# Fused attention and two gated layers on one core: three pairs' first products with v in full fp32, the first pair loaded in one transfer per part, and a new order for attention

## The chip, the cores and the metric

The kernel runs on one core of a Trainium2 chip. The metric is the device time of one execution in microseconds (us), lower is better. It is taken as the median of several runs. The engines are named as in the profile: PE is TensorE (matmuls), PEld its weight loads, DVE is VectorE, ACT is ScalarE, POOL is GpSimd, and SP is SyncE, which here issues nearly all DMA transfers.

## The reference

Attention with a threshold, then a gated layer, then a layer with a cosine:

```
# q, k, v: (batch 4, heads 8, sequence 576, head width 64), fp32
scores = q @ k.T / 8
scores = where(scores >= rowmax(scores) - tau, scores, -1e9)
attn   = exp(scores - rowmax(scores)); attn /= rowsum(attn) + 1e-9
x      = attn @ v                          # laid out as 2304 tokens x 512
x      = (sigmoid(x @ w_gate) * (x @ w_val)) @ w_out      # width 1536
h      = x @ w_in                                          # width 2048
out    = (h * cos(h)) @ w_out2
```

The layers' weights arrive as float64, and the kernel turns their words into fp32 itself.

## The kernel before, in words

Almost every product is made from operands that are split in two: a high part that is rounded to the matmul's own fp32r form, and a low part, which is what the rounding left. High by high, high by low and low by high are then summed in PSUM, so that the result is close to full fp32 without a full fp32 matmul.

**Attention** goes over 16 pairs of heads. For each pair there are nine blocks of 128 query rows, written `Queries` in the code: four blocks of 128 rows for each of the two heads, and one block that joins the last 64 rows of both heads. A block goes through these tasks, each with a letter in the order strings:

- S: PE makes the scores of 128 rows by 576 keys (two or three matmuls for each half of 288 columns).
- M, E, Y, K: DVE takes the row maximum, ACT the exponential, some engine adds the threshold (`YS` says which), DVE masks and sums.
- T and t: PE transposes the result in pieces of 128 by 128, since the product with v wants the keys on the partitions.
- H and h: ACT copies the transposed piece out of PSUM as the high part. H is 512 wide, h is 128 or less.
- the low part, in one of three ways, which `LOWS` and `LOWS_L` choose for each piece. "V": DVE subtracts the high part from PSUM (L, l). "G": ACT copies the piece once more (C), and POOL subtracts (G). "T": PE subtracts the high part inside PSUM by a matmul with minus the identity (N, n), and ACT copies what is left (O, o).

A pair's products with v (`Values`, letter V) come in two blocks of queries (blk 0 with 256 columns, blk 1 with 320) for each of the two heads. Each sums over five slots of 128 keys. Two forms exist, and `SHARED` chooses. In the plain one the high and low columns of v stand side by side in the array, which takes 9 matmuls and leaves two halves that ACT folds (F) and DVE adds (A). In the shared one ("S") they are added in PSUM in 14 matmuls, and one ACT copy (a) takes the result. The fifth slot needs the rest keys' high and low parts stacked on the partitions: four DMA transfers from SP (s) do that. v itself is loaded by SP (2) and split into high and low by Z and z.

When a pair's products are done, x is divided by the row sums (U), stored, and split (X, x). As soon as two pairs of one batch are through, the first layer's products for that batch can begin (letter P, 144 tasks): they are what PE does between the blocks of later pairs.

**The order** of all these tasks on each engine is written out by hand in `ORDER`, one string for each engine. The first pair is loaded by a way of its own (`begin`): q in three parts and k in two, each part by two transfers that put the same rows into the lower and the upper 64 partitions. Before the first scores PE transposes the identity 36 times (`warm`), and four-transpose fillers (letter D, `FILL`) follow a few of the first blocks.

**The layers** follow from about 386 us on; their order is not touched by the change.

## Time and profile before

| | |
|---|---|
| runs | 1092.18, 1090.88 and 1091.71 us: median 1091.71 |
| profiled execution | 1094.26 us, of which the span from first to last instruction is 1092.5 |
| granted TensorE clock | 1.000 over the span |
| PE busy | 1071.8 us, 98% |
| DVE busy | 909.9 us, 83% |
| ACT busy | 764.4 us, 70% |
| POOL busy | 543.7 us, 50% |

The span is about 1.8 us shorter than the profiled execution's own time: that is what lies before the first and after the last instruction. The profiled execution is 2.55 us above the median of the runs. The busy time of PE is modelled from the starts of matmuls that overlap, so a stretch in which PE is 98% busy can still hold small gaps. Attention takes the first 386 us or so, and the two layers the other 706 us.

### The profile page before, as it was taken

The numbers are of one execution on the slowest core, as the hardware profiler recorded it, in microseconds if no ns is written. First come the engines' busy times: TensorE is split into PE (matmuls) and PEld (weight loads), VectorE is DVE, ScalarE is ACT, GpSimd is POOL, SyncE is SP. The second block draws the span as 40 slices with busy tenths as digits, with TensorE's granted clock in tenths as the row PEclk, the third lists the DMA queues.
The fourth block names the chain that finished last, engine by engine and source line by source line (L and its number), as shares of the span: only waits on it lengthen the run. The fifth ranks groups of instructions, "written<-read, shape, count | busy, mean of one in ns | idle before, by whom it ended". The sixth has DMA issues, their size and how long they took to land.

```text
span 1092.5 us, 17726 instructions
## 1 busy us (share of the span) xinstructions
PE 1071.8 (98%) x5784; PEld 912.5 (84%) x5784; DVE 909.9 (83%) x1647; ACT 764.4 (70%) x1488; POOL 543.7 (50%) x521
## 2 busy tenths in 40 slices
PE   8899999999999999999999999999999999999998
PEld 7788898888888888988888888888888888888886
DVE  7999898999888747877787657788779899889998
ACT  6999788887888744656554334367876777788774
POOL 6867877746675525232335252242244535445563
PEclk9999999999999999999999999999999999999999
DMA  7888788787777278998877554866444444557752
GB/s 194 235 225 250 213 225 225 205 232 216 198 207 203 90 231 280 329 331 315 299 228 244 163 191 138 291 203 210 173 154 154 157 175 169 193 193 262 277 203 87
DMA packets 94494, 234.06 MB, mean 214 GB/s; under 512 B 13258, under 2 KB 21570, under 8 KB 84674
## 3 DMA queue, kind: packets, MB, share of 16 engines
q1 hardware_dynamic: 94242, 232.60, 66.7%
q8 instruction: 46, 0.75, 0.3%
q10 hardware_dynamic: 160, 0.33, 0.1%
q14 instruction: 46, 0.38, 0.1%
HBM read 141.33 MB, written 59.84 MB: 184 GB/s over the span
## 4 chain that ended last, share of the span: by engine, by line
PE 51%; DVE 2%; DMA 1%; ACT 1%; issue 0%; ACTq 0%
PE h L1441 5%; PE h L1442 5%; PE h L1443 5%; PE h L1630 4%; PE h L1631 4%; PE h L1632 4%; PE o L1750 4%; PE o L1751 4%; PE o L1752 4%; PE o L565 3%; PE o L566 3%; PE o L564 3%; DMA early<-gd 1%; PE o L1840 1%; PE o L1842 1%; PE o L1841 1%
## 5 line engine op out<-in xcount | busy, mean ns | idle before, releaser
L1676 POOL TENSOR_TENSOR g<-raws,g 128x512 fp32r<-128x512 f32 x68 | 94.7, 1402 | 139.7 <-ACT g L1675 117.6
L965 DVE TENSOR_REDUCE sm<-s 128x1 f32<-128x576 f32 x144 | 106.5, 751 | 8.9 <-PE s L959 7.2
L973 DVE SCALAR_TENSOR_TENSOR p<-s,sm,p 128x576 f32<-128x576 f32 x128 | 102.7, 812 | 9.3 <-ACT p L970 3.9
L1441 PE MATMUL h<-x,w 128*128 128x256 f32 (+1 forms) x304 | 101.4, 333 | 0.4 <-DVE raws L1718 0.4
L1442 PE MATMUL h<-x,w 128*128 128x256 f32 (+1 forms) x304 | 101.3, 333 | 0.0
L1443 PE MATMUL h<-x,w 128*128 128x256 f32 (+1 forms) x304 | 101.3, 333 | 0.0
L970 ACT ACTIVATE p<-s,sm 128x576 f32<-128x576 f32 x128 | 93.8, 742 | 9.8 <-DVE sm L965 9.0
L899 ACT ACTIVATE PT<-t 128x512 fp32r<-128x512 f32 (+1 forms) x160 | 86.1, 557 | 15.1 <-PE t L989 10.3
L959 PE MATMUL s<-kk,qh 128*128 128x288 f32 x320 | 92.4, 320 | 2.9 <-DVE p L973 2.5
L1056 PE MATMUL v<-PT,vn 128*128 128x256 f32 (+3 forms) x532 | 84.7, 302 | 0.2 <-ACT st L1214 0.2
L919 POOL TENSOR_TENSOR PT<-praw,PT 128x512 fp32r<-128x512 f32 x51 | 66.7, 1307 | 35.4 <-ACT praw L914 16.9
L1760 DVE TENSOR_TENSOR y<-o,y 128x512 f32<-128x512 f32 x120 | 78.6, 681 | 6.1 <-PE o L1752 5.9
L959 PE MATMUL s<-khi,ql 128*128 128x288 f32 x288 | 81.0, 295 | 0.6 <-DVE ql L670 0.6
L989 PE MATMUL t<-ident,p 128*128 128x128 f32 x512 | 77.0, 276 | 3.2 <-DVE PT L910 1.7
L1750 PE MATMUL o<-g,w 128*128 128x512 f32 x196 | 76.8, 392 | 0.5 <-ACT o L1766 0.5
L1751 PE MATMUL o<-g,w 128*128 128x512 f32 x196 | 76.4, 390 | 0.0
L1752 PE MATMUL o<-g,w 128*128 128x512 f32 x196 | 76.3, 389 | 0.0
L1630 PE MATMUL h<-form,w 128*128 128x512 f32 x192 | 75.0, 390 | 0.5 <-ACT side L1599 0.5
L1056 PEld LDWEIGHTS v<-PT,vn 128*128 128x128 f32 (+1 forms) x532 | 73.3, 186 | 2.2 <-DVE x L1031 0.5
L1631 PE MATMUL h<-form,w 128*128 128x512 f32 x192 | 74.7, 389 | 0.0
L1632 PE MATMUL h<-form,w 128*128 128x512 f32 x192 | 74.7, 389 | 0.0
L1675 ACT ACTIVATE g<-raws 128x512 fp32r<-128x512 f32 x106 | 64.3, 624 | 13.1 <-DVE raws L1718 8.3
(212 smaller groups left out, 3386.1 us busy)
## 6 DMA issues: line engine op xcount, KB each, us to landing
w<-wd SPq DMA_DIRECT2D x62, 1024.0 KB
wd<-stage SPq DMA_DIRECT2D x64, 512.0 KB
gd<-st SPq DMA_DIRECT2D x64, 256.0 KB
wraw<-in_moe_w_out_dram SPq DMA_DIRECT2D x28, 512.0 KB
qh<-qsplit SPq DMA_DIRECT2D x60, 144.0 KB
wraw<-in_moe_w_in_dram SPq DMA_DIRECT2D x16, 512.0 KB
spare<-gd SPq DMA_DIRECT2D x7, 1024.0 KB
early<-gd SPq DMA_DIRECT2D x7, 1024.0 KB
```

What stands on the lines that cost most here:

```text
L959: nc.tensor.matmul(s[:, half, 0:HALF], qq, keys[:, half * HALF:half * HALF + HALF], start=(i == 0), stop=(i == len(mms) - 1),)
L965: nc.vector.tensor_reduce(self.sm()[:, 0:1], self.s()[:, :, 0:HALF], axis=AX.XY, op=ALU.min)
L1056: nc.tensor.matmul(o, w, x, start=z == 0, stop=z == len(steps) - 1)
L1441: nc.tensor.matmul(o, w_hi, x(0, c), start=begin, stop=False, **late)
L1442: nc.tensor.matmul(o, w_hi, x(1, c), start=False, stop=False, **late)
L1443: nc.tensor.matmul(o, w_lo, x(0, c), start=False, stop=c == KC - 1, **late)
L1630: nc.tensor.matmul(ps(), of(0, c), hi, start=fresh and c == 0, stop=False, skip_group_check=True)
L1631: nc.tensor.matmul(ps(), of(0, c), lo, start=False, stop=False, skip_group_check=True)
L1632: nc.tensor.matmul(ps(), of(1, c), hi, start=False, stop=c == 1, skip_group_check=True)
L1750: nc.tensor.matmul(ps(), of(0, c), hi, start=begin, stop=False, skip_group_check=True)
L1751: nc.tensor.matmul(ps(), of(0, c), lo, start=False, stop=False, skip_group_check=True)
L1752: nc.tensor.matmul(ps(), of(1, c), hi, start=False, stop=True, skip_group_check=True)
```

## The change

- `SHARED` gets a third value, "F". The first two products of the first three pairs (blk 0, both heads) carry it. For them the transposed pieces are copied out of PSUM once, as plain fp32, and no low part is made. The product takes v as it was loaded, unsplit, and is made of five plain fp32 matmuls of 256 columns. It doesn't need the four stacking transfers, and its result is taken by one ACT copy, as in the shared form.
- The tile that v is loaded into gets a second buffer.
- Each part of the first pair's q and k is loaded by one transfer of 128 partitions, from a copy in DRAM that holds the rows twice.
- 26 identity transposes instead of 36 stand before the first scores. Half of the zero fills at the start go to DVE. The second copy of the first pair's keys on POOL waits for the first part of q's low half as well.
- `ORDER`, `LOWS`, `LOWS_L`, `SHARED`, `WHERE`, `YS` and `FILL` are new for all of attention. `WHERE` says for each pair which engine scales, splits and divides.

The count of tasks that change, before and after: PE N 18 to 4, n 3 to 2; ACT O 18 to 4, o 3 to 2, F 59 to 56, a 5 to 8, Y 29 to 36, X 4 to 7; DVE L 91 to 93, l 93 to 88, A 59 to 56, Y 53 to 60, U 2 to 6, q 4 to 6, z 1 to 2; POOL Y 62 to 48, U 15 to 11, X 12 to 9, q 14 to 12; SP s 124 to 112.

```diff
 LOWS = (
-    "TTGTTVTTG VTGVVTVVT GVTTVTGVT VGVVVVGGV GVVVGVTGV VVVGGVGVG GVVGVVGVG GVGVVVVGV "
...
+    "FFFFVTGVG FFFFGVVGT FFFFTVVGV VGVVVVGVV GGVVGVVGV VGVGGVGVG GVGVGVGVV GGVGVVGVV "
...
 LOWS_L = (
-    "TVVV VVTV VVVV VVVV VVVV VVVV VVVV VVVV VVTV VVVV VVVV VVVV VVVV VVVV VVVV VVVV "
+    "VVVT VVVV VVVV VVVV VVVV VVVV VVVV VVVV VVTV VVVV VVVV VVVV VVVV VVVV VVVV VVVV "
 SHARED = (
-    "SSS. .S.S .... .... .... .... .... .... .... .... .... .... .... .... .... .... "
+    "FF.. FF.S FF.. ...S .... .... .... .... .... .... .... .... .... .... .... .... "
 WHERE = dict(
-    Q="APPPPPPPPPAAAPPP", q="DPPPPPPPPPPPPDPP", J="APPPPPPPPAPPPPPP", j="DPPPPPPPPPPDPPPP",
-    Z="PPAPPPPPPPPPPAAP", z="PPPPPPPPPPPPPDPP", s="AAPPPPPPPAPAAPPP", X="PPPPPPPPPPPAAAPA", x="DDPPPPPPPPPPDDDD", U="PPPPPPPPPPPPPPPP",
+    Q="APPAPPPPPPPAPPPP", q="DPPPPDPPPPPDPDPP", J="APPPPPPAPPPPAPPA", j="DPPPDPPPPPPPPPPP",
+    Z="APPPAPPPPPPPPPPA", z="PPPPPDDPPPPPPPPP", s="AAAAPPPPPPPPPPAA", X="PAAPPPPPPAAPAAPA", x="PPPPPPPDDPPPDDDD", U="PDPPPPPPPPPDPDDP",
 YS = (
-    "APPPPDDDD DPPPPPPAA ADPAPADPA DPPDPPPPA PPPDPAPPA DDPDPADPP PPPDPDPDD ADPAAPDPD "
+    "DPPDPDDDA PPPPDDPPD PAPAAPPPP DDAADDDAP ADDPPADPD ADAPPDPDD PDDDDADAD AADAADAAP "
...
-            nc.gpsimd.memset(f32(t), 0.0)
+            (nc.vector if i else nc.gpsimd).memset(f32(t), 0.0)
...
-    for _ in range(36):
+    for _ in range(26):
         nc.tensor.transpose(warm[:, 0:P], ident, ident)
...
+        def exact(self, blk):
+            return SHARED[4 * self.p + 2 * blk] == "F"
...
         def load(self, nm, part=None, queue=nc.sync):
...
-                self.raw[nm] = at.tile([P, src.shape[1]], F32, tag=f"raw_{nm}", name=f"raw_{nm}")
+                self.raw[nm] = at.tile([P, src.shape[1]], F32, tag=f"raw_{nm}", name=f"raw_{nm}", bufs=2 if nm == "v" else 1)
                 queue.dma_start(self.raw[nm], src)
                 return
-            src = self.src[nm][NP].rearrange("(d a) n -> d (a n)", a=2)
-            for i in range(2):
-                queue.dma_start(self.first_raw(nm, part)[64 * i:64 * i + 64], src[:, part])
+            width = src.shape[1]
+            half = part.start // width
+            queue.dma_start(self.first_raw(nm, part), self.src[nm][NP + half][:, part.start - half * width:part.stop - half * width])
...
                 if nm == "k":
                     half["K", i] = task("POOL", pool1(S) + (0.24 if not i else 0.0), "J", lambda r=r: self.first_keys(r), last,
-                                        uses=[*raw, self.khi])
+                                        i and half["q", 0], uses=[*raw, self.khi])
...
             if blk not in pair.LT:
+                kind = F32 if pair.exact(blk) else F32R
...
                 last = task("ACT", act(size) + (0.13 if size < P else 0), high_, high, turn, uses=[bank, to])
-                if by == "G":
+                if pair.exact(blk):
+                    pass
+                elif by == "G":
...
-            self.LZ = pair.LT[blk] if self.close else pair.LZ[blk]
-            lasts = pair.last[blk] if self.close else pair.stacked[blk]
+            self.LZ = pair.LT[blk] if self.close or self.exact else pair.LZ[blk]
+            lasts = pair.last[blk] if self.close or self.exact else pair.stacked[blk]
...
+            if self.exact:
+                raw, steps = self.pair.raw["v"], [(4 * h + c, everything, PT[:, 0, c, 0:n]) for c in range(4)]
+                steps.append((8 + h, one_head, self.LZ()[one_head, 0, 0:n]))
+                for z, (slot, rows, x) in enumerate(steps):
+                    nc.tensor.matmul(o, raw[rows, D * slot - 64 * h:D * slot + D], x, start=z == 0, stop=z == len(steps) - 1)
+                return
```

## Rows read from the trace of the kernel before

**Rows 1.** The page: busy time of the engines, and the granted clock in 40 slices.

```profile
PE 1071.8 (98%) x5784; PEld 912.5 (84%) x5784; DVE 909.9 (83%) x1647; ACT 764.4 (70%) x1488; POOL 543.7 (50%) x521
...
PEclk9999999999999999999999999999999999999999
```

**Rows 2.** Busy us (and count) of PE, PEld, DVE, ACT, POOL by stretch.

```profile
8.00:73.70 65.70, 57.40 (x390) 48.77 (x389) 61.91 (x135) 58.95 (x129) 48.85 (x56) 1.00 0.83 223
73.70:386.00 312.30, 307.85 (x1994) 268.36 (x1993) 278.03 (x645) 263.67 (x574) 202.82 (x236) 1.00 0.73 205
...
386.00:1092.50 706.50, 699.90 (x3369) 588.75 (x3367) 567.97 (x864) 438.28 (x781) 286.35 (x212) 1.00 0.63 218
```

**Rows 3.** Timeline of the start: start, us, engine, instruction.

```profile
0.73 1.19 ACTq L640 DMA_DIRECT2D x<-in_k_dram  x2
...
1.18 1.19 SPq L640 DMA_DIRECT2D x<-in_q_dram  x2
...
1.36 5.51 PE L599 MATMUL warm<-ident 128*128 128x128 f32 x25 [1.36 <-POOL halfpi L477]
...
5.18 0.74 ACT L657 ACTIVATE kk<-x 128x640 fp32r<-128x640 f32 x1 [1.74 <-DMA x<-in_k_dram]
...
5.95 0.82 DVE L674 TENSOR_TENSOR kk<-x,kk 64x640 fp32r<-64x640 f32 x1 [2.33 <-ACT kk L657]
...
6.71 1.36 PE L599 MATMUL warm<-ident 128*128 128x128 f32 x11
...
6.80 0.73 DVE L670 SCALAR_TENSOR_TENSOR ql<-x,taus,qh 64x128 fp32r<-64x128 f32 x1
...
6.87 0.44 SPq L636 DMA_DIRECT2D raw_k<-in_k_dram  x1
...
7.83 0.38 PE L959 MATMUL s<-kk,qh 128*128 128x288 f32 x1
```

**Rows 4.** DVE's groups by form, 0 to 386 us: busy us, mean ns.

```profile
L910 DVE TENSOR_TENSOR PT<-t,PT 128x512 fp32r<-128x512 f32 x65 | 44.5, 685 | 5.8 <-ACT PT L899 5.0
L910 DVE TENSOR_TENSOR LT<-t,LT 128x128 fp32r<-128x128 f32 x61 | 17.2, 281 | 2.7 <-ACT LT L899 2.3
...
L1031 DVE TENSOR_TENSOR x<-v,half 64x256 f32<-64x256 f32 x29 | 12.1, 418 | 0.8 <-ACT half L1026 0.2
L817 DVE TENSOR_SCALAR sm<-sm,taus 128x1 f32<-128x1 f32 x53 | 10.6, 205 | 0.4
...
L910 DVE TENSOR_TENSOR PT<-t,PT 128x256 fp32r<-128x256 f32 x26 | 10.1, 419 | 3.1 <-ACT PT L899 2.8
...
L1169 DVE TENSOR_TENSOR xs_a<-x,xs_a 128x512 fp32r<-128x512 f32 x4 | 2.7, 681 | 0.0
...
L710 DVE TENSOR_TENSOR ql<-raw_q,qsplit 128x576 fp32r<-128x576 f32 x1 | 0.7, 748 | 0.0
```

**Rows 5.** ACT's copy of a T-form low part, 0 to 386 us.

```profile
L906 ACT ACTIVATE PT<-t 128x512 fp32r<-128x512 f32 x12 | 7.2, 599 | 0.1
```

**Rows 6.** Timeline of PE: fillers, one shared product, the first layer product.

```profile
8.44 1.91 PE L825 MATMUL warm<-ident 128*128 128x128 f32 x16
...
30.12 1.61 PE L1056 MATMUL v<-PT,vn 128*64 128x256 f32 x12
31.57 0.39 PE L1056 MATMUL v<-LZ,vn 128*64 128x256 f32 x2
31.80 0.39 PE L903 MATMUL t<-PT,minus_r 128*128 128x512 f32 x1
...
70.84 0.40 PE L564 MATMUL m<-xs_a,w 128*128 128x512 f32 x1
```

**Rows 7.** PEld's groups by form, 0 to 386 us: weight loads.

```profile
L989 PEld LDWEIGHTS t<-ident,p 128*128 128x128 f32 x512 | 59.0, 140 | 16.9 <-DVE PT L910 3.2 <-DVE LT L910 3.0 <-ACT PT L906 0.9
...
L1056 PEld LDWEIGHTS v<-PT,vn 128*64 128x64 f32 x24 | 3.0, 134 | 0.1
```

**Rows 8.** The chain of waits between 375 and 505 us, longest piece.

```profile
487.60 12.15 DMA early<-gd
```

More of the change, by code (lines that the diff above doesn't have):

```diff
@@ L126 @@
 FILL = (
-    "421001001 000000000 000000000 000000000 000000000 000000000 000000000 000000000 "
+    "421100010 000000000 000000000 000000000 000000000 000000000 000000000 000000000 "
     "000000000 000000000 000000000 000000000 000000000 000000000 000000000 000000000 "
@@ L724, in values @@
             p = self.p
-            raw = buf("raw_v")
+            raw = self.raw_v = buf("raw_v", size=2)
             eh, el = either("Z", p), either("z", p)
-            last = task("SP", 0.47, "2", lambda: self.load("v"), uses=[raw], moved=VW)
+            last = self.v_raw = task("SP", 0.47, "2", lambda: self.load("v"), uses=[raw], moved=VW)
             last = task(eh, act(VW, True) if eh == "ACT" else pool1(VW), "Z", lambda: self.hi("v", eh), last, uses=[raw, self.vb])
@@ L751, in begin @@
                 if (nm, i) not in (("q", 0), ("k", 0)):
-                    last = task("SP", 0.94, load, lambda nm=nm, r=r: self.load(nm, r), uses=raw, moved=n)
+                    last = task("SP", 0.57, load, lambda nm=nm, r=r: self.load(nm, r), uses=raw, moved=n)
                 if nm == "k":
                     half["K", i] = task("POOL", pool1(S) + (0.24 if not i else 0.0), "J", lambda r=r: self.first_keys(r), last,
-                                        uses=[*raw, self.khi])
+                                        i and half["q", 0], uses=[*raw, self.khi])
                 last = task("ACT", act(n, True), high, lambda nm=nm, r=r: self.first_hi(nm, r), last, uses=raw + to)
@@ L871, in tasks @@
             if blk not in pair.LT:
+                kind = F32 if pair.exact(blk) else F32R
                 for i in range(2):
                     pair.PT[blk, i] = buf(
-                        f"PT{i}", lambda i=i: at.tile([P, 2, 4, 320], F32R, tag=f"PT{i}", name=f"PT{i}", bufs=2), 2
+                        f"PT{i}", lambda i=i, kind=kind: at.tile([P, 2, 4, 320], kind, tag=f"PT{i}", name=f"PT{i}", bufs=2), 2
                     )
                     pair.ready[blk, i] = []
-                pair.LT[blk] = buf("LT", lambda: at.tile([P, 2, 320], F32R, tag="LT", name="LT", bufs=2), 2)
+                pair.LT[blk] = buf("LT", lambda kind=kind: at.tile([P, 2, 320], kind, tag="LT", name="LT", bufs=2), 2)
                 pair.last[blk] = []
@@ L934, in tasks @@
                     pair.ready[blk, whose].append(last)
-            if j == 2 * blk + 1 and h == 1 and not pair.closing(blk):
+            if j == 2 * blk + 1 and h == 1 and not pair.closing(blk) and not pair.exact(blk):
                 width = 256 + 64 * blk
@@ L1004, in __init__ @@
             self.shared = SHARED[4 * pair.p + 2 * blk + h] == "S"
-            self.PT, self.close = pair.PT[blk, h], pair.closing(blk)
-            self.LZ = pair.LT[blk] if self.close else pair.LZ[blk]
-            lasts = pair.last[blk] if self.close else pair.stacked[blk]
+            self.PT, self.close, self.exact = pair.PT[blk, h], pair.closing(blk), pair.exact(blk)
+            self.shared = self.shared or self.exact
+            self.LZ = pair.LT[blk] if self.close or self.exact else pair.LZ[blk]
+            lasts = pair.last[blk] if self.close or self.exact else pair.stacked[blk]
             self.bank = bank = bank_v()
-            pv = task("PE", products(n, (14 if self.shared else 9) + self.close), "V", self.product, *pair.ready[blk, h],
-                      *lasts, pair.v_done, pvs[0], *(fills if pvs[0] is None else []), uses=[bank, self.PT, self.LZ, pair.vb])
+            of, v = (pair.v_raw, pair.raw_v) if self.exact else (pair.v_done, pair.vb)
+            pv = task("PE", 2.23 if self.exact else products(n, (14 if self.shared else 9) + self.close), "V", self.product,
+                      *pair.ready[blk, h], *lasts, of, pvs[0], *(fills if pvs[0] is None else []), uses=[bank, self.PT, self.LZ, v])
             pvs[0] = pv
@@ L1942, in _two @@
     first = _np.concatenate([t[0, 0], both[0, 1, :, :S + again * SL], t[0, 0, :, :again * SL]], axis=1)
-    return _np.concatenate([whole, first.reshape(1, P, -1)], axis=0)
+    twice = [_np.concatenate([x, x], axis=0)[None] for x in _np.split(first, 2, axis=1)]
+    return _np.concatenate([whole, *twice], axis=0)
 def _values(a):
```

58 lines of the change are left out of this document (29 added, 29 removed).

## The prediction

> **What bounds the kernel now.** I read the page first. PE is busy 98% of the span and the granted clock is full in every slice [rows 1]. So the time is PE's work plus the stretches in which PE is kept waiting, and the question is where those are. The table by stretch answers it [rows 2]. From 386 us on, in the layers, PE is busy 699.9 of 706.5 us, and nothing there is edited. From 73.7 to 386 us it is busy 307.9 of 312.3, with DVE at 89%: PE sets the pace. From 8 to 73.7 us it is busy only 57.4 of 65.7 us, while DVE is busy 61.9 (94%) and ACT 59.0 (90%). That is the first three pairs. The first layer's products, which fill PE's gaps later, don't begin before 70.84 us [rows 6]. Before that PE has nothing to put between two blocks but 36 filler transposes of some 0.12 us each (1.91 us for 16) [rows 6], so about 8.3 us of idle time and 4.3 us of fillers are free on PE. DVE and ACT set the pace of this stretch. The third view is the timeline of the start: the first scores begin at 7.83 us, right behind the last warming transpose and 0.3 us behind the last low part that they need (6.80 + 0.73) [rows 3].
>
> So an edit pays only if it lets the first scores begin sooner, or takes work from DVE and ACT in the first three pairs, or work from PE afterwards.
>
> **The first load.** Each part costs one transfer issue in place of two. Two take 1.19 us on either queue, and one transfer of 128 partitions takes 0.44 us (k of the second pair) [rows 3]. The second of two therefore lies 0.6 us later than it must, and the chain behind it is serial: k lands for ACT at 5.18, then DVE's two low parts follow, then the scores. I take 0.6 us off the start. The bounds are nothing (the bytes are the same, and if moving them is what takes the time, no issue is saved) and 1.1 us, by which the warming ends sooner: 25 transposes take the first 5.3 us and the other eleven 1.1 us, for the engine has gone from 1.2 to 2.4 GHz by then [rows 3]. With 26 the rise is still reached, and PE then waits some 0.4 us for its operands. DVE's new zero fills are three of the short instructions that POOL ran; DVE idles 2.33 us right before its first low part [rows 3] and hides them. Without that cover they would cost about a microsecond. The new wait of POOL's second key copy is for a DVE result of 7.5 us; behind it on POOL stands the second pair's query split, which isn't needed before the first pair is through. I cost it at nothing.
>
> **DVE in the first three pairs**, counted from the strings, with the means of [rows 4]. Low parts of 512: of these pairs' blocks eight are subtracted on DVE before and five after, -3 x 0.685 = -2.06. A joined block moves to DVE, two halves of 256: +2 x 0.419 = +0.84. Low parts of 128: -5 x 0.281 = -1.41. Folded products: seven before, five after, -2 x 0.418 = -0.84. Splits of x: -2 x 0.681 = -1.36. One threshold more, +0.21. One division of x comes from POOL; no row has it on DVE, so I take the split of 128 x 576, +0.75. The sum is -3.9 us; as DVE is busy 94% of this stretch, 3.6 us of time.
>
> **ACT there** loses the copies of the T form: nine of 512 and two of 256, at 0.599 us for 512 [rows 5] and some two thirds of that for 256, near 6.2 us. It takes on two splits of x and a scaling and drops three thresholds, so about 5 us remain as a gain. ACT therefore does not become the bound. Both engines get lighter by about the same share, which is why I let DVE's sum stand.
>
> **PE there.** Nine subtractions of 512 columns and two of 256 go. A shared product of 14 steps takes 1.68 us from 30.12 to 31.80 [rows 6], that is 0.12 us for 256 columns and 0.24 for 512: -2.4 us. The six products were 69 steps of 256 columns (14, 14, 9, 14, 9, 9), -8.3 us. One product of blk 1 goes from 14 steps to 9 of 320 columns at 0.15: -0.7. In their place stand 30 plain fp32 matmuls of 256 columns, and the trace has none. Below, one step of fp32r, 0.12 us, would make 3.6 us. Fp32 transposes take 0.12 for 128 columns [rows 6], 0.24 for 256, 7.2 us in all. Above, a full product has all four partial products of the halves, 4 x 0.12 = 0.48, 14.4 us. I take the upper one, since the split form needs nearly three steps a slot and still leaves one partial product out. PE's balance is +3.0 us (-7.8 at the lower bound). The free 8.3 us of idle time hide it; they, not the fillers, are the cover. If it were gone, the 3.0 us would be added.
>
> The rows on weight loads bear on this too: an fp32 stationary of 128 columns loads in 140 ns for the transposes, and a 64-column half of the split v in 134 [rows 7]. The Trainium skill's page "TensorE: Matmul & The Clock Gate", in the section on fast weight load, says that this mode is off for fp32 operands and measures it at about twice the speed. By that rule each of the 30 loads of raw v could take some 0.13 us more, 4 us in all (an estimate from that page's factor and the 134 ns); no row here shows a weight load of that kind in an ordinary matmul.
>
> **SP and the chain.** Twelve stacking transfers go, so a product waits for ACT's copies and not for a DVE subtraction, an SP issue and a landing behind it. The second buffer of v lets pair 1's load stand before pair 0's last exact product. PE's next stage is not waiting for x before two pairs are through, so I count nothing here beyond DVE's sum; at most this adds 3 us, the waits of PE in the free 8.3 us that T chains and late low parts cause.
>
> **After the first layer product.** PE loses one T subtraction of 512 and two of 256 (-0.5), and gains five steps of 320 in pair 3 (+0.7): +0.2 us. POOL hands work to DVE: counted like above, DVE takes three low parts (+2.06), six thresholds (+1.23), three divisions (+2.24), two splits of x (+1.36), two of q and one of v (+2.25), less one fold (-0.42): +8.7 us on 278.0 [rows 2], or 93% busy in place of 89%. PE's own work hides it as long as the subtractions land ahead of need. I charge 0.5 us for it, with bounds of 0 and 8.7.
>
> **Sum**, against the profiled execution of 1094.26 us (a span of 1092.5 and 1.8 around it): -0.6 - 3.6 + 0.2 + 0.5 = -3.5, so 1090.8. That execution is 2.55 us above the median of the runs, and the difference carries over: 1091.7 - 3.5 = **1088.2 us**, with 1086.6 to 1089.5 as this case's own range (the gain on DVE between 2.3 and 5).
>
> **Rivals.**
>
> *Given back* (1091.1 us). Only the 0.6 us of the start stays. One way: the low parts are merely moved, for up to the mask of the last block of the fourth pair DVE's new string has as much work as the old one, since four more 512-wide low parts stand in the fourth pair's stretch. Against it: by then PE has the first layer's products to run. The other way: attention ends sooner, but the layers wait for what attention stored. The chain of waits has one piece of 12.15 us there, a reload of gd that begins at 487.60 [rows 8]; if transfers and not the engines set that point, 3 us turn into a wait near 500 us. Against it: the transfer's own start hangs on the order that is shifted as a whole.
>
> *DVE becomes the bound later* (slower, 1093.2 to 1096.2 us). Place: 73.7 to 386 us, where the 8.7 us are added. At 94% DVE held PE up in the first stretch, and 93% is near it. It decides from 4.0 us on the path, which undoes the gain, and at 6.2 of the 8.7 us the kernel is slower by more than a measurement can tell. All 8.7 make 1096.2. For it speaks DVE's share, against it that PE there has 64 groups of layer products to fall back on, which the first stretch lacks.
>
> *The fp32 matmul or its weight load costs more than the gap holds.* PE has 8.3 us free and the balance takes 3.0; the gain is gone once the 30 matmuls cost some 9 us more than the upper bound, 0.78 us each. By the weight-load estimate, 4 us, that point is not reached. If no gap lies where the products stand, those 4 and the 3.0 us are exposed: 1095.2 us.
>
> *More than counted* (1085.2 us). The shorter chains to the products also remove PE's waits in the first stretch, 3 us.
>
> **How the numbers follow.** The forecast has 0.53, given back 0.22, DVE later 0.12, the matmul's price 0.05, more than counted 0.08. A difference of 0.2%, 2.2 us, is about what a measurement of this kernel can tell from no change; so faster means under 1089.5. The forecast is faster in nearly all of its range (0.49), the more-than-counted case in full: 0.57. Given back and the small ends of the forecast and of the DVE case make 0.28, and the remaining 0.15 are slower. The range leaves out the far parts of DVE later and of the matmul's price, and the last of the best case: 1084.8 to 1093.4.
>
> **What the profile after would show.** The first scores at 7.2 us. The first layer product at 66.5 us or a little after (70.84 now), with DVE still above 90% before it, and PE's idle time before it down from 8 to below 6 us. 256-column fp32 steps of v about 0.45 us apart. Attention's last product some 3.5 us sooner, and everything behind it unchanged in length. The prediction is wrong if the first layer product comes no sooner, if PE's idle time from there to the end of attention grows from 4.5 us by more than 3, or if a wait near 500 us takes up the lead.

## The result, and the profile after

| | before | after |
|---|---|---|
| median of the runs beside each other | 1091.88 us (1090.88 to 1092.18, 4 runs) | 1097.99 us (1097.36 to 1098.74, 4 runs) |
| ratio | | 1.006, 95% interval 1.0048 to 1.0072 |
| profiled execution | 1094.26 us, span 1092.5 | 1098.34 us, span 1096.4 |

The kernel is 6.1 us slower, 0.6%. The forecast was 1088.2 us in a range of 1084.8 to 1093.4. The two spans differ by 3.9 us only, for the profiled execution of before is a long one (2.4 us above the median in the table).

The page of the changed kernel, to be read beside [rows 1]. Over the whole span PE has 2.3 us more to do and DVE 9.0 us more:

```profile
PE 1074.1 (98%) x5750; PEld 911.4 (83%) x5750; DVE 918.9 (84%) x1658; ACT 762.0 (69%) x1485; POOL 527.1 (48%) x492
```

The table by stretch, with the columns of [rows 2]. The cuts are where DVE begins the mask (K) of the third and of the fifth pair's last block, and where the first of the layers' products begins. In the changed kernel these are 76.3, 128.7 and 389.8 us:

```profile
8.00:76.30 68.30, 58.49 (x362) 47.15 (x362) 60.98 (x128) 55.95 (x120) 44.33 (x52) 0.98 0.72 196
76.30:128.70 52.40, 51.34 (x324) 43.97 (x324) 49.40 (x110) 44.79 (x98) 34.95 (x37) 1.00 0.79 221
128.70:389.80 261.10, 257.69 (x1671) 225.17 (x1669) 235.38 (x550) 219.90 (x483) 155.55 (x178) 1.00 0.71 201
389.80:1096.40 706.60, 700.74 (x3373) 589.70 (x3372) 570.00 (x865) 437.69 (x782) 287.94 (x212) 1.00 0.63 218
```

The same stretches of the kernel before are 8 to 73.7 us (65.7 us long, in [rows 2]), and:

```profile
73.70:122.30 48.60, 47.92 (x316) 41.89 (x315) 45.60 (x103) 43.80 (x95) 36.50 (x45) 1.00 0.80 231
122.30:385.00 262.70, 258.93 (x1676) 225.65 (x1674) 231.95 (x542) 219.44 (x479) 166.32 (x192) 1.00 0.72 202
385.00:1092.50 707.50, 700.90 (x3373) 589.58 (x3372) 568.45 (x864) 438.71 (x782) 286.35 (x212) 1.00 0.63 218
```

By these cuts the time is lost early: 2.6 us in the first three pairs, and 3.8 us in the fourth and fifth (52.4 against 48.6). From there to the end of attention and through the layers nothing more is lost. The second figure depends on the cut, since the two orders have their masks at other places in PE's work: at the mask of the sixth pair's last block the lag is 3.2 us (147.6 and 144.3), at the end of attention 4.8. And some 1 us of the first figure may go with the clock: in this execution the granted clock stood at half for 3.4 us from 58.7 us on, and the two of the four runs with the same mean clock (0.998) took 1.0 us more than the two at 1.000. In the first stretch DVE's work fell by 0.9 us, from 61.91 to 60.98, and yet the stretch got longer: DVE's share went from 94% down to 89%, and PE's idle time up from 8.3 to 9.8 us. In the second stretch PE has 3.4 us more to do and DVE 3.8, and PE is again 98% busy. From 8 us to the end of attention PE is busy 3.3 us longer than before (367.5 and 364.3) and idle 1.5 us longer (14.3 and 12.8): none of its idle time was filled.

The timeline of the start, to be read beside [rows 3]:

```profile
2.59 0.43 SPq L643 DMA_DIRECT2D x<-in_q_dram  x1
...
5.62 1.18 POOL L686 TENSOR_SCALAR khi<-x 64x576 fp32r<-64x576 f32 x3 [2.29 <-DMA x<-in_k_dram]
5.84 0.40 ACT L658 ACTIVATE qh<-x,taus 128x128 fp32r<-128x128 f32 x1 [3.18 <-DMA x<-in_q_dram]
...
6.14 0.72 ACT L660 ACTIVATE kk<-x 128x640 fp32r<-128x640 f32 x1
...
6.87 0.67 POOL L686 TENSOR_SCALAR khi<-bc 64x576 fp32r<-64x576 f32 x1
6.90 1.32 DVE L677 TENSOR_TENSOR kk<-x,kk 64x640 fp32r<-64x640 f32 x1 [0.27 <-ACT kk L660]
...
8.27 0.40 PE L965 MATMUL s<-kk,qh 128*128 128x288 f32 x1 [1.11 <-DVE kk L677]
```

One transfer takes 0.4 us to issue where two took 1.19, but ACT comes to k later than before, at 6.14 us (5.18 before): its string now has the first part of q ahead, which it waits for until 5.84. Nor did k land sooner: POOL waits for it until 5.62, where before ACT had both halves at 5.18. DVE's low part of k, now the last operand of the first scores, takes 1.32 us in place of 0.82, beside the key copy on POOL that began 0.03 us ahead of it. The first scores come at 8.27 us, not at 7.83.

The fp32 product, which no row of before showed (timeline of PE, the first pair's first product):

```profile
27.41 1.94 PE L1053 MATMUL v<-PT,raw_v 128*64 128x256 f32 x8
...
29.28 0.64 PE L1053 MATMUL v<-LT,raw_v 64*64 64x256 f32 x2
...
29.86 0.33 PE L1002 MATMUL t<-ident,p 128*128 128x128 f32 x1
```

Five matmuls stand as ten records. From 27.41 to 29.86 us they take 2.45 us, 0.49 for a step, where the shared product before took 1.68 [rows 6].

### The profile page after: what moved, and what is told of

Its sections match the earlier page's. It is cut to its first block, busy times and chain, and to the rows that moved or that the text cites. A ratio compares the mean times of both kernels' runs of the same rounds, so it can differ in the third digit from the quotient of the medians.

```text
span 1096.4 us, 17558 instructions
## 1 busy us (share of the span) xinstructions
PE 1074.1 (98%) x5750; PEld 911.4 (83%) x5750; DVE 918.9 (84%) x1658; ACT 762.0 (69%) x1485; POOL 527.1 (48%) x492
## 4 chain that ended last, share of the span: by engine, by line
PE 83%; DVE 8%; ACT 3%; DMA 2%; issue 2%; POOL 2%; SPq 0%; DVEq 0%; ACTq 0%; POOLq 0%
PE h L1455 7%; PE h L1456 7%; PE h L1457 7%; PE s L965 6%; PE o L564 5%; PE o L565 5%; PE o L566 5%; PE h L1644 4%; PE h L1645 4%; PE h L1646 4%; PE v L1070 4%; PE o L1764 4%; PE o L1765 4%; PE o L1766 4%; PE t L995 4%; PE m L564 2%
## 5 line engine op out<-in xcount | busy, mean ns | idle before, releaser
L903 ACT ACTIVATE PT<-t 128x512 fp32r<-128x512 f32 (+2 forms) x160 | 85.2, 555 | 13.3 <-PE t L995 11.4
L995 PE MATMUL t<-ident,p 128*128 128x128 f32 x512 | 76.3, 276 | 4.8 <-ACT PT L903 1.7
L529 POOL TENSOR_TENSOR w<-wt,w 128x512 fp32r<-128x512 f32 x30 | 40.6, 1360 | 76.0 <-ACT w L525 74.7
L1766 PE MATMUL o<-g,w 128*128 128x512 f32 x196 | 76.3, 389 | 0.0
L1070 PE MATMUL v<-PT,vn 128*128 128x320 f32 (+1 forms) x472 | 76.0, 304 | 0.1
L995 PEld LDWEIGHTS t<-ident,p 128*128 128x128 f32 x512 | 60.0, 141 | 18.2 <-issue 3.2
## 6 DMA issues: line engine op xcount, KB each, us to landing
qh<-qsplit SPq DMA_DIRECT2D x60, 144.0 KB
```

The costliest lines, as they stand in the source:

```text
L995: nc.tensor.matmul(tp[:, c * P:(c + 1) * P], self.pn[:, k0:k0 + P], ident, is_transpose=True, start=(c == 0), stop=(c == 3))
L1070: nc.tensor.matmul(o, w, x, start=z == 0, stop=z == len(steps) - 1)
L1766: nc.tensor.matmul(ps(), of(1, c), hi, start=False, stop=True, skip_group_check=True)
```

## The experiments

Each run's median is compared with runs of the kernel before on the same chip: 1090.62 us for e1 to e4, 1090.99 for e5 to e8, 1091.49 for e9 to e12, 1090.73 for e13 to e15 and 1091.91 for e16 to e18. "Mask of the third pair" stands for the start of DVE's mask of that pair's last block.

### The parts, one at a time

**e1**, the changed kernel with the old load and 36 warming transposes:

```diff
-    for _ in range(26):
+    for _ in range(36):
...
-            queue.dma_start(self.first_raw(nm, part), self.src[nm][NP + half][:, part.start - half * width:part.stop - half * width])
+            src = self.src[nm][NP].rearrange("(d a) n -> d (a n)", a=2)
+            for i in range(2):
+                queue.dma_start(self.first_raw(nm, part)[64 * i:64 * i + 64], src[:, part])
...
```

> The changed kernel with its first load undone: two transfers for each part of the first pair's q and k again, and 36 identity transposes before the first scores; all else as changed. Load theory (one transfer per part lands later, because the next parts are issued sooner and share the way): most of the 6.1 us comes back, 1092 to 1094 us, and the first scores begin at 7.8 us. Order theory and price theory: the load matters by no more than the 0.4 us by which the first scores were later, 1097.5 to 1098.5 us.

Measured: 1097.93 us, ratio 1.0062 (1.0050 to 1.0074). The old load gives nothing back.

**e2**, the same edit turned around in the kernel before: its order, the new load, 26 transposes.

> The kernel before with the new load alone: one transfer per part, 26 identity transposes. Load theory: slower by several us, 1094 to 1097. My prediction's step: 0.6 us faster, 1091.3. Order and price theory: within 0.7 us of before, on either side.

Measured: 1091.23 us, ratio 1.0005 (0.9996 to 1.0014). The first scores come at 7.31 us, 0.5 sooner than in the profile of before, but that is no gain of the load: with the old load and the old order they come at 7.21 (e3), 7.29 (e18), 7.63 (e5), 7.88 (e10) and 8.08 us (e14), right behind the warming transposes, which end sooner or later from one execution to the next. ACT's wait for k ends at 5.56 us here and at 5.06 to 5.24 in those five and in before: in one transfer k lands 0.3 to 0.5 us later. The first pair's last mask begins at 28.8 us against 28.6. The load costs and brings nothing that can be measured.

**e3**, the kernel before with the six fp32 products alone: its load, its strings with the tasks that fall away dropped.

```diff
 SHARED = (
-    "SSS. .S.S .... .... .... .... .... .... .... .... .... .... .... .... .... .... "
+SHARED = ('FFS.FF.SFF......................................................')
...
+            if self.exact:
+                raw, steps = self.pair.raw["v"], [(4 * h + c, everything, PT[:, 0, c, 0:n]) for c in range(4)]
...
```

> The kernel before with the fp32 products alone: the first two products of the first three pairs are made from unsplit operands, the low parts, stacking transfers and folds that this frees are dropped from the written order, and every other task keeps its place. Price theory (a product that holds PE for 2.4 us, and 14.5 us of PE in place of 8.3, costs more than the freed low parts give back): slower, 1094 to 1097 us. Order theory (the fp32 products are a gain and the new order loses it): faster, 1088 to 1090.5 us. Load theory: as the order theory.

Measured: 1097.84 us, ratio 1.0062 (1.0050 to 1.0074): one part of the change alone costs as much as all of it. Against e2, a profile in the same order, the second pair's mask is not late (49.3 against 49.5 us), the third's is late by 2.3 us and the fourth's by 4.8, and the lag stays there (5.2 at the end of attention). The stretch of the first three pairs in e3, up to its own cut:

```profile
8.00:75.60 67.60, 57.62 (x369) 46.86 (x367) 58.59 (x126) 54.51 (x119) 45.50 (x53) 1.00 0.76 208
```

PE sits idle for 10 us in it, DVE is relieved by 3.3 us against [rows 2], ACT by 4.4, and the kernel is late all the same.

**e4**, the changed kernel with two of the five matmuls in each fp32 product, which leaves out three quarters of the first 512 keys:

```diff
-                steps.append((8 + h, one_head, self.LZ()[one_head, 0, 0:n]))
+                steps = steps[:1] + [(8 + h, one_head, self.LZ()[one_head, 0, 0:n])]
```

> The changed kernel with two of the five matmuls in each fp32 product, so that three quarters of the first 512 keys are left out of six products; PE has 8.7 us less to do in the first three pairs, and every wait stays. Price theory: 1091 to 1093 us. Order and load theory: PE wasn't what the first pairs waited for, 1096 to 1098 us.

Measured: 1098.24 us, ratio 1.0076 (1.0064 to 1.0089). 7.8 us less work on PE brings nothing. (A product now takes 1.15 us in place of 2.45, 1.3 us less in each of six; the 8.7 us expected were 18 times the mean step, but a step on all 128 rows takes only 0.43 us.) The granted clock takes a share of it: its mean was below 1 in all six runs, and the time goes with it (1097.51 us at a mean of 0.998 over the run, 1100.53 at 0.991, 1101.76 at 0.988). The changed kernel's own two runs at 0.998 took 1098.34 and 1098.74, so at a like clock e4 gains about 1 us.

**e5**, the edit of e4 in e3:

> The order and the load of before with the six full fp32 products, but each of them with two of its five matmuls; this leaves out three quarters of the first 512 keys of the products, so the output is another. The work of PE falls by 18 x 0.48 = 8.7 us against the products alone in before's order (1097.8 us), to 5.9 us for the six where the split steps took 8.3. Theory of the price (in that order the time of the products is paid where they stand): 1088 to 1091 us, no longer than before. Rival (the steps, splits and copies that fell out, or the waits for them, set the time, not the matmuls): it stays at 1096 to 1098 us.

Measured: 1090.62 us, ratio 1.0003 (0.9992 to 1.0014). All of the price is gone. With e3 and e4 this says: in the old order the time of the products is paid nearly one for one (7.8 us of PE against 7.2 us of time), in the new order hardly at all. The changed kernel is slow for another reason than e3. The stretch of the first three pairs in e5:

```profile
8.00:73.00 65.00, 54.09 (x347) 43.29 (x346) 59.10 (x126) 54.29 (x119) 45.14 (x53) 1.00 0.81 217
```

Against [rows 2] PE has 3.3 us less to do, DVE 2.8 and ACT 4.7, and the stretch is 0.7 us shorter (0.2 against e2, with 65.2).

### Other orders

**e6, e7, e8**: the work of the changed kernel, of before and of e3, with the strings of `ORDER` rearranged by a search over the task costs that the kernel's planner carries (the start of DVE's string in e6):

```diff
-    DVE=(
-        "qjMjYqKqMMKKM4Y5KMMKYKMYLK4MlYMlK5K...
...
+    DVE='jqqqMjYK4MMKKM5YKMMKYKM4YMKL5MYllKK...
```

> The changed kernel with all its work, engine for engine, as it is (the fp32 products, the one-transfer load, who subtracts, copies and splits what); only the order of the engines' strings is another, which moves the fp32 products, the low parts and the first layer products against each other. Theory of the order: at or below before's time, under 1092 us, with the mask of the fourth pair's last block nearer to 94.9 us than to 102.5. Rival (the products, or DVE's larger load after the third pair, cost the time whatever the order): 1096 to 1099 us.

> Before's work, engine for engine, in another order of the strings, found in the same way as that of the reordered changed kernel. It says what an order alone is worth where nothing else is changed. Theory of the order: it is worth several microseconds, 1085 to 1090 us, and the reordered changed kernel lies within 2 us of it. Rival (the products cost time whatever the order): the reordered changed kernel stays 5 us or more above it.

> Before's assignment of work and its load, with the six fp32 products in place of the split ones, in another order of the strings. In before's own order this change cost 6.6 us. Theory of the order: the price is that of products set into an order made for others, so this lies within 2 us of before's work reordered. Rival (the price is the matmuls'): it stays 5 us or more above that.

Measured: 1131.83, 1130.28 and 1119.04 us, ratios 1.0381 (1.0367 to 1.0395), 1.0367 (1.0350 to 1.0385) and 1.0262 (1.0248 to 1.0276). Both theories expected a better order, and none of these is one, so they don't tell the theories apart. They show one thing: with not a single task changed, the order alone moves the time of before by 39 us, six times the loss to be explained. In e7 the granted clock stands at half (1.2 of 2.4 GHz) for 27 us in all, ten of them in the second of the page's 40 slices:

```profile
PEclk9899999999999999999999999999999999999999
```

### DVE beside POOL

The timeline of the changed kernel has pairs of rows like these (POOL's and DVE's alone, some left out):

```profile
24.94 1.42 POOL L713 TENSOR_TENSOR ql<-raw_q,qsplit 128x576 fp32r<-128x576 f32 x1
...
25.18 1.46 DVE L517 TENSOR_SCALAR wt<-wraw 128x512 uint32<-128x512 uint32 x1
...
29.14 1.27 POOL L923 TENSOR_TENSOR PT<-praw,PT 128x512 fp32r<-128x512 f32 x1 [1.08 <-ACT praw L918]
...
29.26 1.70 DVE L520 SCALAR_TENSOR_TENSOR wt<-we,wt 128x512 uint32<-128x512 uint32 x1
...
50.49 1.54 POOL L713 TENSOR_TENSOR ql<-raw_q,qsplit 128x576 fp32r<-128x576 f32 x1 [0.64 <-ACT qsplit L706]
...
50.87 1.72 DVE L520 SCALAR_TENSOR_TENSOR wt<-we,wt 128x512 uint32<-128x512 uint32 x1
...
60.72 0.69 DVE L520 SCALAR_TENSOR_TENSOR wt<-we,wt 128x512 uint32<-128x512 uint32 x1
60.73 1.94 POOL L1161 TENSOR_TENSOR x<-x,bc 128x576 f32<-128x576 f32 x1
```

The two instructions that turn the weights' words take 0.42 and 0.69 us. One that begins while a long POOL instruction is running takes up to 1.0 us more: it ends 0.3 to 0.6 us after POOL's does. At 60.72 DVE is first by 0.01 us, takes its 0.69, and POOL's instruction is the long one. In the changed kernel DVE is held up so five times before 90 us, for 4.7 us together. In the kernel before it is two, for 1.2 us. The Trainium skill's page "SBUF — State Buffer", in its section "Who interferes with whom", says that DVE and GpSimd share one pair of ports under an exclusive lock, and that whichever of two such instructions comes second is blocked until the first is through. The trace agrees, with 1.70 us at 29.26 for DVE second and 1.94 us at 60.73 for POOL second.

**e9** writes POOL's subtractions in attention, and those of the weights' first twelve pieces, as two shorter instructions of one operand, which leaves these low parts out; **e10** does so in the kernel before; **e11** is e9 with the short products of e4; **e12** leaves nothing out and moves three of DVE's instructions by one or two places.

```diff
+    def two(to, src):
+        for _ in range(2):
+            nc.gpsimd.tensor_scalar(to, src, 0.0, 0.0, op0=ALU.mult, op1=ALU.add)
...
-            eng = nc.vector if engine == "DVE" else nc.gpsimd
-            eng.tensor_tensor(to, raw, f32(hi), op=ALU.subtract)
+            if engine == "DVE":
+                nc.vector.tensor_tensor(to, raw, f32(hi), op=ALU.subtract)
+            else:
+                two(to, raw)
...
```

```diff
-        "qjMjYqKqMMKKM4Y5KMMKYKMYLK4MlYMlK5KlMLM4KKIMM5KKMYM4YKKMA5KLMLAM4Y5KLKlIlMMllKKM45KMMKKAMM4KKU5LLMllMKKLl45M"
-        "MYYKLjMlIKK4ML5MKYKMMYYlKL45lKLMAMKLLLK4AllM5MlqYKLLMK45IAlYKMMAKlLMlKKLMYMAKKLLlMlMYLKlAKAMLlMYIKKLMMKKMMYl"
+        "qjMjYqKqMMKKM4Y5KMMKYKMY4LKMlYMlK5KlMLM4KKIMM5KKMYM4YKKMA5KLMLAM4YKL5KlIlMMllKKM45KMMKKAMM4KKU5LLMllMKKLlMM4"
+        "5YYKLjMlIKK4ML5MKYKMMYYlKL45lKLMAMKLLLK4AllM5MlqYKLLMK45IAlYKMMAKlLMlKKLMYMAKKLLlMlMYLKlAKAMLlMYIKKLMMKKMMYl"
```

> The changed kernel, but each of POOL's subtractions of two operands from SBUF in attention (low parts of q, k, v, p, x and of the first twelve pieces of the weights) is written as two instructions of one operand, which take POOL about as long (two of 0.72 us where one of 576 to 640 columns took 1.4 to 1.6). This leaves out these low parts (zeros in their place). In the profile after, five of DVE's shift and merge instructions on the weights run beside such a subtraction before 90 us and take 1.0 to 1.7 us in place of 0.42 and 0.68, 4.7 us together, where before loses 1.2 us in two. Theory of the collisions (the new order lays DVE's instructions beside POOL's, and DVE paces the first five pairs): 1092.5 to 1095 us, and these instructions all at 0.42 and 0.68 us. Rival (the order's loss lies in the waits between PE, ACT and DVE): 1097 to 1098.5 us.

> The same edit in the kernel before, the same low parts left out. Theory of the collisions: 1089.5 to 1091 us, for only 1.2 us of DVE's time is lost there. If it gains as much as the changed kernel does, POOL's subtractions cost both kernels the same and the collisions explain nothing.

> The changed kernel with POOL's one-operand instructions and also with two of the five matmuls in each fp32 product (low parts and three quarters of the first 512 keys of the products left out). If DVE's collisions hid the price of the products in the changed kernel, taking out both gives more than the collisions alone: 1088 to 1091 us. Rival (the products' time is hidden in the new order whatever DVE does): the same time as with POOL's edit alone, within 1 us.

> The changed kernel with nothing left out; only DVE's string has three edits of one to two places: one shift instruction earlier (25.2 us), two merge instructions later (50.9 and 78.3 us), into stretches in which POOL runs no subtraction. Theory of the collisions: up to 3 us back where the moved instructions meet no other subtraction, 1095 to 1097 us. Rival: 1098 us.

Measured:

| | us | ratio |
|---|---|---|
| e9 | 1095.41 | 1.0040 (1.0027 to 1.0053) |
| e10 | 1091.76 | 1.0003 (0.9994 to 1.0011) |
| e11 | 1094.58 | 1.0030 (1.0018 to 1.0041) |
| e12 | 1097.42 | 1.0051 (1.0039 to 1.0063) |

e9 gives back 2.6 us of the 6.1 by the bare medians (0.4 less than the theory's worst), and 2.2 if each kernel is set against the runs of before beside it; e10 gives back nothing. So POOL's long instructions cost the new order something that they don't cost the old. The meetings didn't vanish: in e9 they are shorter (3.3 us of the 4.7 are gone), since POOL's instructions are half as long; that they have one operand doesn't keep them from holding DVE up.

```profile
25.08 0.64 DVE L521 TENSOR_SCALAR wt<-wraw 128x512 uint32<-128x512 uint32 x1
...
28.73 1.64 POOL L496 TENSOR_SCALAR PT<-praw 128x512 fp32r<-128x512 f32 x2 [0.99 <-ACT praw L927]
...
28.98 0.91 DVE L524 SCALAR_TENSOR_TENSOR wt<-we,wt 128x512 uint32<-128x512 uint32 x1
```

e12 takes nearly all of the long ones before 90 us away (0.4 us of 4.7 is left), more than e9, and gains only 0.6 us, with intervals that overlap: inconclusive on its own. Its fifth pair's mask is 1.5 us earlier, and the end of the span 0.9. By these profiles a microsecond that DVE loses this way is worth a third of one or less; that the meetings with DVE are the whole of what e9 gives back is not shown. e11 repeats e4's answer: short products bring 0.8 us.

### What DVE's time is worth

**e13** is e9 with work of DVE in the first six pairs done by POOL again; **e14** and **e15** make DVE's 128-wide low parts of the first five pairs twice, in before and after.

```diff
-            (nc.vector if i else nc.gpsimd).memset(f32(t), 0.0)
+            nc.gpsimd.memset(f32(t), 0.0)
...
-        engine = nc.vector if eu == "DVE" else nc.gpsimd
+        engine = nc.vector if eu == "DVE" and pair.p > 5 else nc.gpsimd
...
```

```diff
-                    nc.vector.tensor_tensor(d[:, 1], src(), f32(d[:, 0]), op=ALU.subtract)
+                    for _ in range(2 if size == P and pair.p in (0, 1, 2, 3, 4) else 1):
+                        nc.vector.tensor_tensor(d[:, 1], src(), f32(d[:, 0]), op=ALU.subtract)
```

> The changed kernel with POOL's subtractions in attention as two one-operand instructions (their low parts left out, 1095.4 us) and in addition the work that the new order moved from POOL to DVE in the first six pairs given back to POOL at the same places: three zero fills (1.25 us of DVE), one low part of k (1.08), one of q (0.75), one division of x (0.76), 3.8 us of DVE together. Theory that DVE's sum sets the pace: 1091.5 to 1093 us. Rival (the rest of the loss is the weave of PE, ACT and DVE): 1095 us, within 0.8.

> The kernel before with nothing left out; the 17 subtractions of 128 columns that DVE makes on the last keys' probabilities in the first five pairs are each made twice, 17 x 0.28 = 4.8 us more on DVE, each ahead of a product that waits for it. If DVE's time there is the kernel's time, as the prediction took it: 1096 us (+4.8). If PE's is, and DVE has slack: 1091 to 1092.5 us.

> The same in the changed kernel, where there are 12 of them, 3.4 us more on DVE. If the new order is paced by DVE, 1101 us or more (+3.4), and more for each microsecond than in the kernel before. If not: 1098 to 1099 us.

Measured: e13 1094.52 us, ratio 1.0037 (1.0024 to 1.0049), no different from e9. It is a weak test: of the 3.8 us, 1.25 are zero fills before the first scores, and 1.4 went into new meetings with POOL, which now had that work, so that from 8 us to the sixth pair's mask DVE is busy 1.5 us less than in e9 (123.96 and 125.44). e14 1094.47 us, 1.0035 (1.0022 to 1.0047): the trace has 18 doubled instructions, one more than counted, and these 5.0 us more on DVE cost 3.7. Its third pair's mask, behind eight of them (2.2 us), is 2.8 us later than before; the next eight, up to the fifth pair's mask, add 0.9. e15 1101.93 us, 1.0105 (1.0089 to 1.0120): 13 doubled instructions, 3.6 us, cost 3.9 over the changed kernel's 1097.99, or 5.1 if each is set against the runs of before beside it. Work *added* to DVE in these pairs costs some 0.7 us for each in the old order and 1.1 or more in the new.

**e16, e17, e18**: the fourth and fifth pairs' 512-wide low parts on DVE cut to 128 columns (the others left out; the products read the high part in their place), in e9, in e11 and in e10.

```diff
...
-                    nc.vector.tensor_tensor(d[:, 1], src(), f32(d[:, 0]), op=ALU.subtract)
+                    if size == 512 and pair.p in (3, 4):
+                        nc.vector.tensor_tensor(d[:, 1, 0:1], src()[:, 0:1], f32(d[:, 0, 0:1]), op=ALU.subtract)
+                    else:
+                        nc.vector.tensor_tensor(d[:, 1], src(), f32(d[:, 0]), op=ALU.subtract)
...
```

> The changed kernel with POOL's one-operand instructions (1095.4 us), and in the fourth and fifth pairs DVE subtracts only the first 128 of each 512 columns of low parts (11 subtractions at 0.28 in place of 0.685 us, 4.4 us less on DVE); the products there read the high part in place of the rest, so that PE's steps stay as they are. This leaves out those low parts. Theory that PE and DVE are both full there, so that one alone gives little: 1094 to 1095.4 us. Rival (DVE's work alone is the rest of the loss): 1091 to 1092.5 us.

> The same with two of the five matmuls in each fp32 product (three quarters of the first 512 keys of these products left out too), which alone was worth 0.8 us (1094.6). Theory that PE and DVE are both full there: together they give what neither gives alone, 1090.5 to 1092.5 us. Rival (neither is the limit, the waits of the weave are): 1094 to 1095 us.

> The kernel before with POOL's one-operand instructions (1091.8 us) and the same short low parts in its fourth and fifth pairs, 9 of them, 3.6 us less on DVE. If PE alone paces that stretch before, as the prediction read it: 1091 to 1092 us. If DVE does: 1088 to 1089 us.

Measured: e16 1095.43 us, ratio 1.0030 (1.0021 to 1.0040); e17 1094.78, 1.0027 (1.0016 to 1.0037); e18 1091.86, 0.9997 (0.9988 to 1.0006). Work *taken* from DVE in the fourth and fifth pairs brings nothing that can be told from no change in either order: 4.0 us of it (ten instructions, one fewer than counted) bring 0 to 1 us, 3.6 us bring none. e17, which relieves PE and DVE together, keeps 3 us of the loss by its median, but its clock was lower: its runs have means of 0.995 to 0.998, those of e16 0.997 to 1.000. At 0.997 and 0.998 its four runs took 1093.56 to 1094.44 us, six of e16 1093.68 to 1096.81 and four of before, beside them, 1091.91 to 1093.88. At a like clock e17 is therefore on the mean 1.7 us faster than e16 and 1.1 us slower than before. So the theory that PE and DVE are both full there is neither shown nor refuted. The stretch of these two pairs in e9, e16 and e17 (the last with the one ahead of it):

```profile
73.60:125.10 51.50, 51.22 (x323) 43.94 (x323) 48.48 (x110) 44.78 (x98) 33.92 (x54) 1.00 0.81 227
```

```profile
73.50:124.40 50.90, 50.59 (x321) 43.55 (x321) 45.68 (x113) 44.34 (x97) 34.21 (x53) 1.00 0.82 233
```

```profile
52.00:75.50 23.50, 20.89 (x115) 17.98 (x115) 18.90 (x42) 19.30 (x44) 14.31 (x25) 0.80 0.74 200
75.50:126.10 50.60, 48.59 (x308) 41.57 (x308) 45.37 (x113) 44.21 (x97) 33.89 (x53) 1.00 0.81 229
```

In e9 and e16 PE is idle for 0.3 us in the stretch: it is full. In e17, with shorter products, it idles 2.0 us and the stretch is hardly shorter, though no engine is full; before needs 48.6 us. And ahead of it the clock stood at half for 10.2 us from 51.2 us on (0.80 on the mean from 52 to 75.5), after a stretch of 22 us in which PE had been busy for 17.28 only; the mask of the third pair came 1.9 us later than in e9.

## Why the prediction was wrong

Two steps failed, and one term was missing: work taken from DVE in the first three pairs was counted as time (-3.6 us) and gave none; the 3.0 us that PE gets in addition were to vanish in its idle time and did not; and the new order, taken at nothing, cost several microseconds.

**First load, -0.6 us.** Measured: nothing, by e1 and e2. The issue is shorter, as counted, but k lands 0.3 to 0.5 us later and not 0.6 sooner; the lower bound of the step, nothing, was the right one. The 7.31 us of e2 lie near the 7.2 of the forecast by luck: the old load has 7.21 in one profile. What holds the transfer back is not shown. POOL's second key copy, costed at nothing, ran beside DVE's low part of k in the new order and stretched it by 0.5 us.

**DVE in the first three pairs, -3.9 us of work, "3.6 us of time".** This is the first step that failed. The work went down, though by less than counted: by 0.9 us in the profile after [rows 2], and by 2.3 us between e10 and e9 (61.52 to 59.18), where most of the meetings with POOL are taken out. I had taken durations from means that hold as long as POOL is quiet, and had not asked what POOL runs beside them in the new order. Far worse is the step from work to time. e5 shows it in the old order: with 2.8 us less on DVE, and less on PE and ACT too, the stretch of the first three pairs is 0.2 to 0.7 us shorter. So at 94% DVE was not what set the pace of the stretch, though work added to it there was paid in full (e14, 2.8 us for 2.2). The reading that fits is a ring with PE and ACT (scores, maximum, exponential, mask, transpose, copy), in which an addition is paid and a relief of one station is not (e16 and e18, in the fourth and fifth pairs); no run shows which wait it is that stays.

**PE's balance, +3.0 us, "the free 8.3 us of idle time hide it".** This is the step that failed in full. Its size was right: the upper bound of 0.48 us a step came out at 0.49. In the order that I had read the idle time from, nothing hid it: e3 pays 7.2 us over before, and e5 gets them back. In the changed kernel PE's idle time before the third pair's mask went from 8.3 up to 9.8 us, not below 6. The likely reason, which no run isolates: a product of 2.45 us stands in one piece between scores that DVE is about to need, and idle time in small pieces elsewhere doesn't take it in. The rival in which the price is exposed was the right mechanism for that order, with 1095.2 us too small and a chance of 0.05 far too small.

**The new order.** There was no term for it; I took it as neutral, and counted what moved. In it the products are no longer what is waited for (e4, e11: about 1 us of 7.8). Of its loss, 2.2 to 2.6 us went with POOL's long instructions (e9). In e9 nearly all that remains lies, by these cuts, in the fourth and fifth pairs, 51.5 us against 48.7 in e10. There PE is full, and the third pair's two products (4.9 us of the 14.7 that all six take) run there, not in the stretch whose idle time was to hide them. But at the next cut, the sixth pair's mask, e9 is level with e10 (144.0 and 144.4 us), and at the end of attention it is 3.6 us late, so the cuts don't tell the place. The sums to the end of attention, e9 and then e10, tell more:

```profile
8.00:386.70 378.70, 366.60 (x2353) 315.15 (x2353) 341.59 (x786) 320.60 (x697) 228.18 (x378) 1.00 0.73 205
8.00:383.10 375.10, 362.93 (x2379) 316.50 (x2377) 337.82 (x778) 322.11 (x701) 243.67 (x407) 1.00 0.75 210
```

PE is idle as long in both (12.1 and 12.2 us) and busy 3.7 us longer in e9, which is its balance of the forecast (+3.0 and +0.2), unhidden. That this is the cause is argued, not shown, for shortening the products in e11 turned into idle time (16.8 us to the end of attention) and not into speed; in e17, with DVE relieved too, the loss at a like clock is down to 1.1 us. What holds the new order up by these last 3 to 4 us stays open: the sums of PE and DVE together, or how the tasks are woven.

**After the third pair.** "Given back" had the right place: DVE has 3.8 us more to do in the fourth and fifth pairs. But e16 shows that this isn't the price. "DVE later" fell: from the fifth pair's mask on, DVE works 3.4 us more (231.95 to 235.38), and the stretch is no longer (261.1 us; 262.7 in the long execution of before, 261.1 in e10) and PE no longer idle in it (3.4 us; 3.8 and 3.4).

**The weight-load rule.** The Trainium skill's page "TensorE: Matmul & The Clock Gate", in its section on fast weight load, would, as the prediction read it, have made each load of raw v about 0.13 us longer than the 134 ns of the split half. The trace after doesn't show that price. That section of the Trainium skill asks for a weight of the full 128 columns as well, so the 64-column half was no case of it, and the estimate did not follow. A load of raw v, of 64 or 128 columns, takes 132 to 192 ns (the 64-column ones 136 on the mean); there are two for each step, 0.33 us by the median, and the 0.43 to 0.49 us of the step's two matmul records cover them:

```profile
L1053 PEld LDWEIGHTS v<-PT,raw_v x48: 132/163/192, 27.4 to 84.6; 128*64 128x64 f32 x24, 128*128 128x128 f32 x24
```

**The layers** kept their length (707.5 and 706.6 us), as forecast; that a wait near 500 us would take up a lead was not put to the test, since there was no lead. Of the three signs that were to prove the forecast wrong one came, the first: the first layer product came no sooner, at 73.82 us (70.84 before [rows 6]). PE's idle time behind it did not grow (1.1 and 3.4 us, 4.5 as before). Two sums of the prediction are off by 0.2 us, and nothing hangs on them: 5 us of gain on DVE make 1086.8 and not 1086.6, and all 8.7 us of "DVE later" make 1096.4 and not 1096.2.

## What to carry to other kernels

The idle time of an engine, summed over a stretch, doesn't show that added work will be hidden: here none of it was, so test an addition by its place, not by the stretch's total. Busy shares near 95% don't say that relief pays; here work added to such an engine cost nearly all of itself, and work taken from it, at other places, gave next to nothing. A changed order is a change with a price of its own, and part of it sits in durations: look for instructions of one form that are longer than their fellows, and for what ran beside them. And where an edit lowers the clock, compare runs at a like clock before saying that it gained nothing.

## What the runs showed of the hardware

- A plain fp32 matmul of 256 columns stands as two records and two weight loads. A product of five takes 2.45 us, 0.49 for each, and one of two 1.15 (e5), so that a step on all 128 rows takes 0.43 us, three and a half times a step of the split form (0.12 us).
- DVE's shift and merge on 128 x 512 words in SBUF, begun during a POOL instruction of 1.2 to 1.5 us, last until that one is over: 1.46 and 1.70 us in place of 0.42 and 0.69. If DVE is first by 0.01 us, POOL waits (1.94 us). Masks and maxima, which read PSUM, kept their 0.81 and 0.75 us beside POOL's subtractions.
- Less work on PE can cost clock. The granted clock has the levels 2.4 and 1.2 GHz, and its mean over a run was 0.998 to 1.000 in the changed kernel and 0.988 to 0.998 with short products (e4); 0.997 to 1.000 in e16 and 0.995 to 0.998 with short products beside it (e17). In e9 and e11 it was 0.997 to 1.000 alike. In the profile of e17 it stood at 1.2 GHz for 10.2 us before the layers, in that of e11 and of the changed kernel for 3.4.
- Two transfers of 64 partitions, issued in 1.19 us, had the first part of k ready for ACT at 5.06 to 5.24 us in six profiles of the old order; one transfer of 128 partitions, issued in 0.41 us, had it ready at 5.56 (e2).
